# A convolution branch whose first transform stage goes from 128-row matmuls to pairs of 64-row matmuls, and whose middle stage goes from 16 points over four frequencies to 32 points over two

## The chip, the cores and the metric

The kernel runs on one core of a Trainium2 chip. The metric is the time of one execution on the device in microseconds (us). Three executions of the kernel before took 1200.62, 1201.41 and 1201.98 us; the median, 1201.41 us, is the time that the changed kernel is held against. The core has a matrix engine (TensorE, PE in the rows, with its weight loads listed as PEld), a vector engine (DVE), a scalar engine (ACT), GpSimd (POOL) and a sync engine (SP), which here only issues transfers. The matrix engine holds a weight block of up to 128 rows by 128 columns, streams a moving operand past it and adds the products into a bank of PSUM. Each engine works through its own instructions in order and waits on semaphores for the others.

## The reference: what is computed

The input x has 2048 positions and 576 channels. Four layers are applied, A, B, A, B, each as x + layer(layernorm(x)):

```python
def _A_ref(x, ...):                      # real part of a 2-D DFT, as matmuls
    a, b = x @ hid_re.T, x @ hid_im.T
    return seq_re @ a - seq_im @ b

def _B_ref(q, k, v, shift_k, ssm_k, ssm_D):
    k_shift = short causal convolution of k (4 taps per channel)
    kv = k_shift * v
    y = long causal convolution of kv with ssm_k, per channel, 2048 taps (by FFT)
    return q * (y + kv * ssm_D)
```

In layer B only q, the normalized x, depends on the layers before. kv, ssm_k and ssm_D are inputs, and both B layers use the same ones. So the long convolution ("the branch") is worked out once, from the inputs alone, and both B layers read its result.

## The kernel before

Every float32 operand of a matmul is split into a rounded high part and a low remainder (`split`: ACT writes the high part, line 91, and DVE the low part, line 92). Each product is three matmuls: high by high, high by low, low by high. All go through the helper `mm`, line 74, so that rows of PE all name L74.

**The main line.** The first layer A runs in `layer` over 128 steps (g, tb, k): real or imaginary sequence matrix, one of four blocks of 512 output positions, one of 16 blocks of 128 input positions. A step is 14 matmuls with 512 moving columns: 12 into four banks named s (four channel blocks, three matmuls each) and 2 into the bank rm for the last 64 channels. Its matrix block (`c_mat`, 256 KB) is loaded two steps ahead and split by ACT and DVE. In the first 16 steps x is normalized too (`get_x0`, ACT, DVE and a power on POOL). After each pair of g the channel transform runs (`hidden`, `finish`), 27 matmuls of 288 columns to a half row block. A second layer A follows, part of it by a seven-product scheme (`strassen`), and its channel transform ends the program.

**The branch** (`branch`, a generator) is interleaved with the steps of the first layer A. It has four stages:

1. the short convolution and the product with v on DVE (`convolve`, lines 386 and 391, and line 419);
2. the first transform stage (`f1_products`). Position n is written 16p + j, with p the partition and j one of 16 residues. For each j and each of two sources (kv and ssm_k) the 128 values over p are multiplied by a 128 x 128 cosine matrix and a 128 x 128 sine matrix, in two halves of 288 channels. That gives 128 frequencies in real and imaginary part, for each residue. The result is copied from PSUM by ACT (line 436) and stored to DRAM, `t_d`, by ACT's queue (line 437);
3. the middle stage (`mid_*`): 64 times, 128 rows of `t_d` are loaded (four frequencies, 16 residues, two parts), a 16-point transform over the residues is applied as one block-diagonal 128 x 128 matrix, the spectrum of kv is multiplied by that of ssm_k, and an inverse 16-point transform is applied and stored to `v_d`;
4. the last transform stage (`i2_products`): 32 times, 128 frequencies back to 128 positions, to `yb_d`.

Stage 2 has 32 units (16 j by 2 sources). A unit has two halves of the channels, and a half has two banks, c = 0 for cosine and c = 1 for sine, with three matmuls of 288 columns in each and a copy by ACT behind each:

```python
for c in range(2):
    ps = bank()
    mm(ps[:, :HD], fc[:, c, :], xf[0][:, cs], True, False)
    mm(ps[:, :HD], fc[:, c, :], xf[1][:, cs], False, False)
    mm(ps[:, :HD], fc[:, 2 + c, :], xf[0][:, cs], False, True)
    stored[:] = [nc.scalar.activation(so[:, c, :], ps[:, :HD], AF.Copy).ins]
```

The banks come from a ring of three (`bank`), which the channel transform and the other stages of the branch use as well. The units are doled out over the steps 0 to 42 of the first layer A by a fixed formula (`want`, from `F1_16` and `F1_END`); each unit is named in the program behind a step, and a scheduler in the build mixes the matmuls of neighbouring parts. The weights `fc` of a unit (256 KB for each j) come through POOL's queue (line 165) into a ring of five; the first one comes through SP's queue as float32 (lines 408 and 409). Loads of `c_mat`, x, k, v and ssm_k go through SP's queue. All constants are made on the host by `_constants`, and `kernel` lays the inputs out.

Of the kernel before, what the change touches and what calls it, by code (L numbers as in the profile page):

```python
# [10 lines left out]
F32 = mybir.dt.float32  # L11
FR = mybir.dt.float32r
AF = mybir.ActivationFunctionType
OP = mybir.AluOpType

P = 128
S = 2048
D = 576
J = S // P
TB = 4  # L20
NT = 512
HD = D // 2
NC = 4
REM = D - NC * P
EPS = 1e-5
# [22 lines left out]
KP = 4  # L48
H = 2 * P
WIDE = 2 * NT  # L50
# [14 lines left out]
def fnet_h3_kernel(ctx: ExitStack, tc: tile.TileContext, x, c_mat, w_re, w_im, k_pad, v, shift_k,  # L65
                   ssm_k, ssm_d, f1c, i2c, midc, out):
    nc = tc.nc
# [3 lines left out]
    dr = ctx.enter_context(tc.tile_pool(name="dr", bufs=1, space=bass.MemoryType.DRAM))  # L71

    def mm(ps, lhsT, rhs, first, last, more=False):
        nc.tensor.matmul(ps, lhsT, rhs, start=first, stop=last, skip_group_check=more)  # L74

    def bank():
        return psp.tile([P, NT], F32, tag="b", bufs=3, name="bk")

    acc4 = [psp.tile([P, NT], F32, tag=f"s{i}", name=f"s{i}") for i in range(4)]
    last_pair = [acc4[2:]]  # L80
# [24 lines left out]
    def flat(words, dt, name):  # L105
        return sb.tile([P, words], dt, tag=name, name=name)

# [3 lines left out]
    def region_b(dt, name):  # L111
        return sb.tile([P, 6 * WIDE], dt, tag="rb", name=name)
# [9 lines left out]
    ring = {}  # L122

    def lay(t, at, *sizes):

        for name, words, n in sizes:
            ring.setdefault(name, Ring()).tiles.extend(t[:, at + i * words:at + (i + 1) * words] for i in range(n))
            at += n * words
        assert at <= t.shape[1], (at, t.shape, sizes)
        return at  # L130
# [5 lines left out]
    def two(v):  # L136
        return v.rearrange("p (a n) -> p a n", a=2)
# [17 lines left out]
    anchor, made, rounded, pows, biased, halved, added, evac, parted, stored = [], [], [], [], [], [], [], [], [], []  # L155
# [3 lines left out]
    def load_after(dst, src):  # L159
        with tc.issue_after(anchor[-1]):  # L160
            return nc.sync.dma_start(dst, src).ins

    def load_fr(dst, src):
        with tc.issue_after(pows[-1]):
            nc.gpsimd.dma_start(dst, src)
# [25 lines left out]
        made.append(nc.vector.tensor_tensor(t[:, D + REM:], y[:, :NC * P], h[:, :NC * P], OP.subtract).ins)  # L191
        return t

    t_d = [dr.tile([P, J, 2, 2, HD], F32, name=f"t{h}") for h in range(2)]
    v_d = [dr.tile([P, J, 2, HD], F32, name=f"vd{h}") for h in range(2)]
    yb_d = [dr.tile([P, D], F32, name=f"yb{j}") for j in range(J)]
    xa_d = [dr.tile([P, D], F32, name=f"xa{j}") for j in range(J)]
# [141 lines left out]
    def quads(v):  # L339
        return v.rearrange("p (a q) -> p a q", a=4)  # L340

    def branch():
        f1r = region_b(FR, "f1r")
        lay(f1r, 0, ("xf", 2 * D, 3), ("fc", 4 * P, 5))
        at = lay(flts, SC_AT + CRAW * NT, ("so", D, 4), ("land", D, 3))
        lay(flts, at, ("craw", NT, 1))
        f1f = region_a(F32, "f1f")
        ks = f1f[:, :KR * 2 * D]
        lay(f1f, KR * 2 * D, ("wt", 2 * D, 2), ("rp", 2 * D, 2))
        tmp = f1f[:, 8 * 2 * D:]  # L350
        wt, rows, landed, fcs = [], {}, {}, {}
# [9 lines left out]
        def load_k(upto):  # L361
            while k_loaded[0] < min(upto, (J + 4) // 2):
                i = k_loaded[0]
                at = i % KR * 2 * D
                nc.sync.dma_start(ks[:, at:at + 2 * D],
                                  bass.AP(tensor=k_pad.tensor, offset=k_pad.offset + 2 * i * D,
                                          ap=[[J * D, P], [1, 2 * D]]))
                k_loaded[0] += 1

        def k_rows(row):  # L370
# [27 lines left out]
        def f1_loads(upto):  # L398
            while loads[0] < min(upto, len(todo)):
                j, src = todo[loads[0]]  # L400
                loads[0] += 1
                if j not in fcs:
                    fcs[j] = quads(ring["fc"]())
                    if pows:
                        load_fr(fcs[j], f1c[j])
                    else:
                        raw = quads(tmp[:, :4 * P])
                        nc.sync.dma_start(raw, f1c[j])
                        nc.scalar.activation(fcs[j], raw, AF.Copy)
                landed[j, src] = ring["land"]()  # L410
                nc.sync.dma_start(landed[j, src], (ssm_k if src else v)[:, j, :])
                if src and j == 0:
                    nc.sync.dma_start(tmp[:1, D:], ssm_d[None, :])
# [13 lines left out]
        def f1_products(j, src, xf, fc):  # L427
            for hf in range(2):
                so = two(ring["so"]())
                cs = slice(hf * HD, (hf + 1) * HD)  # L430
                for c in range(2):
                    ps = bank()
                    mm(ps[:, :HD], fc[:, c, :], xf[0][:, cs], True, False)
                    mm(ps[:, :HD], fc[:, c, :], xf[1][:, cs], False, False)
                    mm(ps[:, :HD], fc[:, 2 + c, :], xf[0][:, cs], False, True)
                    stored[:] = [nc.scalar.activation(so[:, c, :], ps[:, :HD], AF.Copy).ins]  # L436
                nc.scalar.dma_start(t_d[hf][:, j, :, src, :], so)
                yield

        conv, made_ops, split_up = convolve(), 0, []  # L440
        for n, (j, src) in enumerate(todo):
            f1_loads(n + 1)
            if n < 2:
                yield
            split_up.append((j, src, f1_split(j, src), fcs[j]))
            products = f1_products(*split_up.pop(0)) if len(split_up) > (1 if n < F1_LAG else 2) else iter(())
            if n:
                f1_loads(n + 3)
            later = [m for m in range(n + 1, len(todo)) if todo[m][1] == 0 and 7 * (todo[m][0] // 2 + 1) > made_ops]
            for half in range(2):  # L450
                next(products, 0)
                if later and n > 2:
                    left = 7 * (todo[later[0]][0] // 2 + 1) - made_ops
                    for _ in range(-(-left // (2 * (later[0] - n) - half)) if left > 0 else 0):
                        next(conv)
                        made_ops += 1
                yield
        next(conv, 0)
        for left_over in split_up:
            yield from f1_products(*left_over)  # L460
        m1 = region_b(FR, "mid")
        kk_at = SC_AT + CRAW * NT + 4 * D
        at = lay(m1, 0, ("df", 2 * D, 3), ("mc", 4 * P, 1))
# [6 lines left out]
        at = lay(m1, at, ("yf", D, 2))  # L470
        fc_at = at
        at = lay(flts, SC_AT + CRAW * NT, ("res", D, 2))
# [76 lines left out]
        rows = [f[2] for f in feeds if f[0]]  # L549
        landed, halves, fcs, yfs = {}, {}, {}, []  # L550

        def load_feed(i):
            if i < len(feeds):
                kind, hf, q = feeds[i]
                landed[i] = ring["land"]()
                load_after(landed[i], v_d[hf][:, q].rearrange("p c d -> p (c d)") if kind else
                           t_d[hf][4 * q:4 * q + 4].rearrange("q j c s d -> (q j c) (s d)"))

        def load_fc(k):
            if k < len(rows):  # L560
# [10 lines left out]
        for i in range(3):  # L571
            load_feed(i)
        yield 0
        for i in range(2):
            split_feed(i)
            load_feed(i + 3)
# [173 lines left out]
    for n, whole in layer(get_x0, lambda j: x[:, j, :], done0, pending):  # L750
# [3 lines left out]
        if (whole or whole is not None and n % J < J - 1) and n <= F1_END and not part:  # L754
            at = n if whole else n - 0.5
# [25 lines left out]
        m = n - PREP  # L781
# [138 lines left out]
    cs, done = {}, []  # L920
# [68 lines left out]
    for n, whole in layer(get_x1, lambda j: xb_d[j], done1, pending, 1):  # L989
# [12 lines left out]
        if n == STATIC:  # L1002
            t7.append(region_a(FR, "t7"))
            at = lay(flts, SC_AT + CRAW * NT, ("csum", WIDE, 3), ("rems", 2 * REM, 2))
# [50 lines left out]
def _r11(a):  # L1055
    u = np.ascontiguousarray(a, np.float32).view(np.uint32).astype(np.uint64)
    u = (u + 0x7FF + ((u >> 12) & 1)) & 0xFFFFF000
    return u.astype(np.uint32).view(np.float32)


def _parts(a):
    h = _r11(a)
    return h, _r11(a - h.astype(np.float64))


def _constants():
    p, q, j, r = np.arange(P), np.arange(P), np.arange(J), np.arange(J)
    n = (16 * p[None, :, None] + j[:, None, None]) * (4 * q[None, None, :] + 1) % 8192
    ang = 2 * np.pi * n / 8192
    f1 = [_parts(np.cos(ang)), _parts(-np.sin(ang))]  # L1070
    f1c = np.stack([f1[0][0], f1[1][0], f1[0][1], f1[1][1]], axis=2)
    at = ang.transpose(0, 2, 1)
    i2 = [_parts(np.cos(at) / S), _parts(-np.sin(at) / S)]
    i2c = np.stack([i2[0][0], i2[1][0], i2[0][1], i2[1][1]], axis=2)
    th = 2 * np.pi * (j[:, None] * r[None, :] % J) / J
    f2 = np.zeros((4, J, 2, 2, 4, J))
    i1 = np.zeros((2, 4, J, 4, J, 2))
    c, s = np.cos(th), np.sin(th)
    for a in range(4):
        f2[a, :, 0, 0, a, :] = c  # L1080
        f2[a, :, 1, 0, a, :] = s
        f2[a, :, 0, 1, a, :] = -s
        f2[a, :, 1, 1, a, :] = c
        i1[0, a, :, a, :, 0] = c.T
        i1[1, a, :, a, :, 0] = -s.T
        i1[0, a, :, a, :, 1] = s.T
        i1[1, a, :, a, :, 1] = c.T
    m = [*_parts(f2.reshape(P, P)), *_parts(i1.reshape(P, P))]
    return f1c, i2c, np.stack(m, axis=1)

# [35 lines left out]
```

## Time and profile before

| | |
|---|---|
| median of three executions | 1201.41 us (1200.62 to 1201.98) |
| the profiled execution, first to last instruction | 1198.9 us |
| its granted matrix clock | 0.998 of full speed |
| PE busy | 1178.8 us, 98% of the span, 6320 matmuls |
| PEld busy | 1025.6 us, 86% |
| DVE busy | 839.6 us, 70% |
| ACT busy | 665.4 us, 55% |
| first transform stage, first to last matmul | 6.8 to 200.8 us |

The profiled execution's own time, as far as the page gives it, is its span of 1198.9 us; the median of the executions is 2.5 us above that. A row of the groups view names the line, engine and operation, then output <- inputs, the tile and the shapes with the count, then busy time in us and mean duration of one in ns, then the engine's idle time ahead of these instructions with what ended most of it. Matmuls are pipelined: a matmul's duration reaches from its start until its result is out, and the next one starts long before that. So the spacing of starts, not the duration, says what a matmul costs in a row of them. In the timeline a row is start, length and a run of like instructions (x9: nine of them).

### The profile page before, as it was taken

Reading aid. Unit: us, or ns where it says so; the run is one execution under the profiler, and the core shown is the slowest. Engines: PE = TensorE matmul, PEld = TensorE weight load, DVE = VectorE, ACT = ScalarE, POOL = GpSimd, SP = SyncE. Lnnn points to the kernel's source line nnn. Section 1 sums busy time; section 2 is a strip of 40 time slices with the busy share of each in tenths; the row PEclk is TensorE's granted clock in tenths of the full one; section 3 lists DMA queues with packets and bytes.
Section 4 is the critical chain, followed back from the end, with each engine's and each line's share of the span. In section 5 each row is a group of like instructions: output and inputs, shape, how many; then the busy total and the mean of one; then the engine's idle time right before and its main releaser. Section 6 shows DMA issues by size and latency. Waiting matters only on the chain.

```text
span 1198.9 us, 18258 instructions
## 1 busy us (share of the span) xinstructions
PE 1178.8 (98%) x6320; PEld 1025.6 (86%) x6320; DVE 839.6 (70%) x1498; ACT 665.4 (55%) x1335; POOL 74.7 (6%) x116
## 2 busy tenths in 40 slices
PE   7999999999999999999999999999999999999997
PEld 6888888988888888888988898888888888789997
DVE  7899983679777677675347766775776777774764
ACT  7855665679877668774435666544444445450210
POOL 2210000000000000001101121000000000001111
PEclk9999999999999999999999999999999999999999
DMA  9869898546766667648967686872682677795621
GB/s 356 292 225 311 282 299 243 188 133 184 219 188 199 213 172 210 193 134 267 291 207 233 221 255 212 272 267 71 216 283 72 208 285 260 238 338 156 218 88 40
DMA packets 146110, 261.95 MB, mean 218 GB/s; under 512 B 15841, under 2 KB 44769, under 8 KB 146018
## 3 DMA queue, kind: packets, MB, share of 16 engines
q1 hardware_dynamic: 102674, 205.58, 53.9%
q10 hardware_dynamic: 36432, 42.63, 10.2%
q0 software_dynamic: 6912, 12.59, 3.9%
q8 instruction: 49, 0.80, 0.3%
q14 instruction: 43, 0.35, 0.1%
HBM read 194.09 MB, written 66.65 MB: 217 GB/s over the span
## 4 chain that ended last, share of the span: by engine, by line
PE 89%; ACT 4%; DVE 3%; DMA 2%; issue 2%; POOL 0%; ACTq 0%; SPq 0%; POOLq 0%; DVEq 0%
PE s L74 50%; PE bk L74 34%; PE rm L74 5%; ACT flts L490 2%; ACT mid L490 1%; DMA flts<-in_c_mat 1%; DVE mats L92 0%; ACT mats L91 0%; ACT u L91 0%; DMA flts<-in_ssm_k 0%; DMA ph<-in_c_mat 0%; DMA wd<-w 0%; DVE u L92 0%; DVE mid L496 0%; DVE f1f L386 0%
## 5 line engine op out<-in xcount | busy, mean ns | idle before, releaser
L74 PE MATMUL s<-mats 128*128 128x512 f32 x2088 | 535.0, 391 | 1.2 <-DVE u L92 0.5
L74 PEld LDWEIGHTS s<-mats 128*128 128x128 f32 x2088 | 380.0, 188 | 70.1 <-DVE u L92 1.1
L92 DVE TENSOR_TENSOR mats<-flts,mats 128x512 fp32r<-128x512 f32 x206 | 140.9, 688 | 63.8 <-ACT mats L91 63.3
L91 ACT ACTIVATE mats<-flts 128x512 fp32r<-128x512 f32 x206 | 128.5, 628 | 84.5 <-PE bk L74 32.3
L74 PEld LDWEIGHTS bk<-mid 128*128 128x128 f32 x768 | 116.2, 188 | 21.7 <-ACT flts L490 8.1
L74 PE MATMUL bk<-mid 128*128 128x288 f32 x768 | 132.5, 299 | 2.2 <-ACT flts L490 2.0
L74 PE MATMUL bk<-w,u 128*128 128x288 f32 x864 | 120.9, 296 | 0.3 <-ACT flts L490 0.3
L74 PEld LDWEIGHTS bk<-w,u 128*128 128x128 f32 x864 | 117.4, 188 | 4.0 <-ACT flts L490 1.9
L496 DVE TENSOR_TENSOR mid<-flts,mid 128x576 fp32r<-128x576 f32 (+1 forms) x149 | 93.5, 628 | 35.2 <-ACT mid L490 32.7
L490 ACT ACTIVATE flts<-bk 128x288 f32<-128x288 f32 x160 | 62.2, 405 | 90.1 <-PE bk L74 81.0
L74 PE MATMUL rm<-mats 128*128 128x512 f32 x304 | 94.9, 391 | 0.0
L490 ACT ACTIVATE flts<-flts 64x288 f32<-64x288 f32 x192 | 85.0, 443 | 5.5
L490 ACT ACTIVATE mid<-flts 128x576 fp32r<-128x576 f32 (+1 forms) x148 | 80.3, 575 | 6.0 <-DMA flts<-t 3.0
L436 ACT ACTIVATE flts<-bk 128x288 f32<-128x288 f32 x128 | 49.3, 410 | 49.9 <-PE bk L74 41.3
L74 PE MATMUL bk<-f1r 128*128 128x288 f32 x384 | 64.2, 300 | 7.7 <-ACT f1r L91 7.6
L74 PEld LDWEIGHTS bk<-f1r 128*128 128x128 f32 x384 | 59.0, 191 | 14.8 <-ACT f1r L91 8.6
L280 DVE TENSOR_TENSOR flts<-flts,bk 128x288 f32<-128x288 f32 x48 | 21.8, 453 | 67.6 <-PE bk L74 67.6
L74 PE MATMUL bk<-mats 128*128 128x288 f32 (+1 forms) x376 | 67.8, 317 | 0.0
L74 PEld LDWEIGHTS rm<-mats 128*128 128x128 f32 x304 | 56.9, 188 | 12.3 <-DVE flts L266 0.3
L74 PE MATMUL s<-t,mats 128*128 128x512 f32 x264 | 64.9, 389 | 0.0
L177 POOL TENSOR_TENSOR flts<-flts 128x1 f32<-128x1 f32 x35 | 29.4, 841 | 522.2 <-DVE flts L176 522.2
L74 PE MATMUL bk<-mats,t 128*128 128x288 f32 (+1 forms) x368 | 59.3, 303 | 0.0
(145 smaller groups left out, 1505.4 us busy)
## 6 DMA issues: line engine op xcount, KB each, us to landing
flts<-in_c_mat SPq DMA_DIRECT2D x148, 256.0 KB, 3.8
ph<-in_c_mat SPq DMA_DIRECT2D x54, 512.0 KB, 4.5
t<-flts ACTq DMA_DIRECT2D x64, 288.0 KB, 4.5
flts<-in_c_mat SPq DMA_DIRECT2D x30, 512.0 KB, 5.3
flts<-t SPq DMA_DIRECT2D x53, 288.0 KB, 2.9
vd<-flts ACTq DMA_DIRECT2D x64, 144.0 KB, 2.3
flts<-vd SPq DMA_DIRECT2D x32, 288.0 KB, 4.5
mid<-in_i2c POOLq DMA_DIRECT2D x32, 256.0 KB, 4.9
```

What stands on the lines that cost most here:

```text
L74: nc.tensor.matmul(ps, lhsT, rhs, start=first, stop=last, skip_group_check=more)
L91: a = nc.scalar.activation(h, src, AF.Copy).ins
L92: return a, nc.vector.tensor_tensor(l, src, h.bitcast(F32), OP.subtract).ins
L177: pows.append(nc.gpsimd.tensor_tensor(rs, ve, mhalf, OP.pow).ins)
L280: added[:] = [nc.vector.tensor_tensor(r[:, cs], r[:, cs], ps[:, :HD], OP.add).ins]
L436: stored[:] = [nc.scalar.activation(so[:, c, :], ps[:, :HD], AF.Copy).ins]
L490: last_act.append(nc.scalar.activation(*args, **kw).ins)
L496: nc.vector.tensor_tensor(l, src, h.bitcast(F32), OP.subtract)
```

## The change

Stage 2 now writes the position as n = 32p + w, with p from 0 to 63 and 32 residues w. For each residue the transform has 64 points: 64 rows are contracted, and the 128 output columns hold 64 frequencies in real and imaginary part. Two residues, j and j + 16, stand in the lower and the upper 64 partitions of the same tile: the host puts the rows of k, v and ssm_k in that order (`by_half`). A half of a unit is now six matmuls of 64 rows, 128 weight columns and 288 moving columns. They alternate between rows 0 to 63, with sums in one bank, and rows 64 to 127, with sums in another; the two banks are taken together, and both copies by ACT come behind the six matmuls. The count of matmuls, copies and stores stays as it was. In the build the matmuls of 64 rows carry a tile size of 64 x 128 and a tile position of row 0 or row 64; all the others carry 128 x 128 at row 0.

The weights of a unit halve from 256 to 128 KB. `t_d` has its 32 residues in place of 16 residues by two parts; a store writes as many rows of the same length, further apart, and a load of the middle stage reads the same number of rows as before. The middle stage covers two frequencies with 32 residues and two parts, again 128 rows, so that only the contents of its matrices change. The last stage reads its frequencies in another order, which is put into its constants. k is stored with its overlapping rows written out, so that a plain slice reads it.

```diff
-    t_d = [dr.tile([P, J, 2, 2, HD], F32, name=f"t{h}") for h in range(2)]
+    t_d = [dr.tile([P, 2 * J, 2, HD], F32, name=f"t{h}") for h in range(2)]
...
-        lay(f1r, 0, ("xf", 2 * D, 3), ("fc", 4 * P, 5))
+        lay(f1r, 0, ("xf", 2 * D, 3), ("fc", 2 * P, 5))
...
-                    fcs[j] = quads(ring["fc"]())
+                    fcs[j] = two(ring["fc"]())
                     if pows:
                         load_fr(fcs[j], f1c[j])
                     else:
-                        raw = quads(tmp[:, :4 * P])
+                        raw = two(tmp[:, :2 * P])
                         nc.sync.dma_start(raw, f1c[j])
...
                 so = two(ring["so"]())
                 cs = slice(hf * HD, (hf + 1) * HD)
-                for c in range(2):
-                    ps = bank()
-                    mm(ps[:, :HD], fc[:, c, :], xf[0][:, cs], True, False)
-                    mm(ps[:, :HD], fc[:, c, :], xf[1][:, cs], False, False)
-                    mm(ps[:, :HD], fc[:, 2 + c, :], xf[0][:, cs], False, True)
-                    stored[:] = [nc.scalar.activation(so[:, c, :], ps[:, :HD], AF.Copy).ins]
-                nc.scalar.dma_start(t_d[hf][:, j, :, src, :], so)
+                ps = [bank() for _ in range(2)]
+                for n, (a, b) in enumerate(((0, 0), (0, 1), (1, 0))):
+                    for i in range(2):
+                        rows = slice(i * HP, (i + 1) * HP)
+                        mm(ps[i][:, :HD], fc[rows, a, :], xf[b][rows, cs], n == 0, n == 2)
+                for i in range(2):
+                    stored[:] = [nc.scalar.activation(so[:, i, :], ps[i][:, :HD], AF.Copy).ins]
+                nc.scalar.dma_start(t_d[hf][:, j::J, src, :], so)
...
-                           t_d[hf][4 * q:4 * q + 4].rearrange("q j c s d -> (q j c) (s d)"))
+                           t_d[hf][4 * q:4 * q + 4].rearrange("m j s d -> (m j) (s d)"))
...
-    n = (16 * p[None, :, None] + j[:, None, None]) * (4 * q[None, None, :] + 1) % 8192
-    ang = 2 * np.pi * n / 8192
-    f1 = [_parts(np.cos(ang)), _parts(-np.sin(ang))]
-    f1c = np.stack([f1[0][0], f1[1][0], f1[0][1], f1[1][1]], axis=2)
+    n = (32 * (p % HP) + J * (p // HP))[None, :, None] + j[:, None, None]
+    ang = 2 * np.pi * (n * (4 * q[None, None, :HP] + 1) % 8192) / 8192
+    f1 = _parts(np.stack([np.cos(ang), -np.sin(ang)], axis=3).reshape(J, P, P))
+    f1c = np.stack(f1, axis=2)
...
+    def by_half(m):
+        return m.reshape(HP, 2, *m.shape[1:]).transpose(1, 0, *range(2, m.ndim + 1)).reshape(m.shape)
...
-        "v": a["B_v"].reshape(P, J, D),
+        "v": by_half(a["B_v"].reshape(P, J, D)),
...
-        "ssm_k": a["B_ssm_k"].T.reshape(P, J, D),
+        "ssm_k": by_half(a["B_ssm_k"].T.reshape(P, J, D)),
```

More of the change, by code (lines that the diff above doesn't have):

```diff
@@ L16 @@
 P = 128
+HP = P // 2
 S = 2048
@@ L364, in load_k @@
                 at = i % KR * 2 * D
-                nc.sync.dma_start(ks[:, at:at + 2 * D],
-                                  bass.AP(tensor=k_pad.tensor, offset=k_pad.offset + 2 * i * D,
-                                          ap=[[J * D, P], [1, 2 * D]]))
+                nc.sync.dma_start(ks[:, at:at + 2 * D], k_pad[:, 2 * i * D:2 * (i + 1) * D])
                 k_loaded[0] += 1
@@ L1066, in _constants @@
 def _constants():
-    p, q, j, r = np.arange(P), np.arange(P), np.arange(J), np.arange(J)
+    p, q, j = np.arange(P), np.arange(P), np.arange(J)
+    n = (32 * (p % HP) + J * (p // HP))[None, :, None] + j[:, None, None]
+    ang = 2 * np.pi * (n * (4 * q[None, None, :HP] + 1) % 8192) / 8192
+    f1 = _parts(np.stack([np.cos(ang), -np.sin(ang)], axis=3).reshape(J, P, P))
+    f1c = np.stack(f1, axis=2)
     n = (16 * p[None, :, None] + j[:, None, None]) * (4 * q[None, None, :] + 1) % 8192
-    ang = 2 * np.pi * n / 8192
-    f1 = [_parts(np.cos(ang)), _parts(-np.sin(ang))]
-    f1c = np.stack([f1[0][0], f1[1][0], f1[0][1], f1[1][1]], axis=2)
-    at = ang.transpose(0, 2, 1)
+    at = (2 * np.pi * n / 8192).transpose(0, 2, 1)
+    at = at[:, np.concatenate([[2 * g, 2 * g + 1, HP + 2 * g, HP + 2 * g + 1] for g in range(HP // 2)])]
     i2 = [_parts(np.cos(at) / S), _parts(-np.sin(at) / S)]
     i2c = np.stack([i2[0][0], i2[1][0], i2[0][1], i2[1][1]], axis=2)
-    th = 2 * np.pi * (j[:, None] * r[None, :] % J) / J
-    f2 = np.zeros((4, J, 2, 2, 4, J))
-    i1 = np.zeros((2, 4, J, 4, J, 2))
+    w = np.arange(2 * J)
+    th = 2 * np.pi * (w[:, None] * w[None, :] % (2 * J)) / (2 * J)
+    f2 = np.zeros((2, 2, 2 * J, 2, 2, 2 * J))
+    i1 = np.zeros((2, 2, 2 * J, 2, 2, J, 2))
     c, s = np.cos(th), np.sin(th)
[L1079 to L1087, printed above, removed]
+    for a in range(2):
+        f2[a, 0, :, 0, a, :] = c
+        f2[a, 1, :, 0, a, :] = s
+        f2[a, 0, :, 1, a, :] = -s
+        f2[a, 1, :, 1, a, :] = c
+    th = 2 * np.pi * (j[:, None] * j[None, :] % J) / J
+    c, s = np.cos(th), np.sin(th)
+    for a in range(2):
+        for b in range(2):
+            i1[0, a, b::2, b, a, :, 0] = c
+            i1[1, a, b::2, b, a, :, 0] = -s
+            i1[0, a, b::2, b, a, :, 1] = s
+            i1[1, a, b::2, b, a, :, 1] = c
     m = [*_parts(f2.reshape(P, P)), *_parts(i1.reshape(P, P))]
@@ L1107 @@
         "w_im": a["A_dft_hid_im"].T,
-        "k_pad": np.pad(a["B_k"][0], ((3, 1), (0, 0))),
-        "v": a["B_v"].reshape(P, J, D),
+        "k_pad": by_half(np.stack([np.pad(a["B_k"][0], ((3, 1), (0, 0)))[J * p:J * p + J + 4].reshape(-1)
+                                   for p in range(P)])),
+        "v": by_half(a["B_v"].reshape(P, J, D)),
         "shift_k": a["B_shift_k"].T,
-        "ssm_k": a["B_ssm_k"].T.reshape(P, J, D),
+        "ssm_k": by_half(a["B_ssm_k"].T.reshape(P, J, D)),
         "ssm_d": a["B_ssm_D"],
```

## The prediction

> **What bounds the kernel now.** I read the page first: the engines' shares and the slices.
>
> ```profile
> PE 1178.8 (98%) x6320; PEld 1025.6 (86%) x6320; DVE 839.6 (70%) x1498; ACT 665.4 (55%) x1335; POOL 74.7 (6%) x116
> ...
> PE   7999999999999999999999999999999999999997
> ...
> DVE  7899983679777677675347766775776777774764
> ```
>
> PE is at work through the whole span, DVE for about two thirds of it. But DVE stands at 8 or 9 in slices two to six (30 us each), and that is where the first transform stage lies. The chain of work that ended last says whether PE's time is the path:
>
> ```profile
> PE 89%; ACT 4%; DVE 3%; DMA 2%; issue 2%; POOL 0%; ACTq 0%; SPq 0%; POOLq 0%; DVEq 0%
> ```
>
> It is, for 89%. So a microsecond of PE added to any stage, or taken from it, is about a microsecond of time, as long as no other engine runs full in that stage. Next the stage itself, by windows, first of all instructions and then of those that touch the branch's tile f1r (columns: PE, PEld, DVE, ACT, POOL in us with counts, clock, DMA share, GB/s):
>
> ```profile
> 15.00:90.00 75.00, 74.24 (x355) 61.59 (x354) 66.81 (x131) 57.79 (x121) 13.85 (x18) 1.00 0.83 287
> 90.00:180.00 90.00, 89.99 (x487) 78.48 (x487) 82.77 (x98) 53.77 (x121) 3.69 (x7) 1.00 0.94 297
> 180.00:202.00 22.00, 22.00 (x123) 19.40 (x122) 7.45 (x11) 13.74 (x31) 0.53 (x1) 1.00 0.76 219
> ```
>
> ```profile
> 15.00:90.00 75.00, 14.01 (x81) 12.35 (x81) 4.51 (x6) 4.07 (x6) 2.69 (x5) 1.00 0.83 287
> 90.00:180.00 90.00, 37.01 (x228) 34.65 (x229) 16.18 (x22) 14.20 (x21) 3.69 (x7) 1.00 0.94 297
> 180.00:202.00 22.00, 9.39 (x60) 8.82 (x60) 1.75 (x3) 1.35 (x2) 0.00 (x0) 1.00 0.76 219
> ```
>
> PE is busy throughout, at full clock. DVE is busy 66.81 + 82.77 = 149.6 of the 165 us from 15 to 180 us, so a faster PE finds 15.4 us of idle DVE there and no more; from 180 us on DVE is free. 309 of the stage's 384 matmuls stand in the tight part, 60 in the free one.
>
> **What a matmul costs today.** Groups by shape, two pieces of the chain, and the timeline of PE and of its loads:
>
> ```profile
> L74 PE MATMUL s<-mats 128*128 128x512 f32 x2088 | 535.0, 391 | 1.2 <-DVE u L92 0.5 <-ACT mats L188 0.3 <-DVE mats L191 0.3
> ...
> L74 PE MATMUL bk<-f1r 128*128 128x288 f32 x384 | 64.2, 300 | 7.7 <-ACT f1r L91 7.6
> ...
> L74 PEld LDWEIGHTS bk<-f1r 128*128 128x128 f32 x384 | 59.0, 191 | 14.8 <-ACT f1r L91 8.6 <-ACT flts L436 1.1
> ```
>
> ```profile
> 146.98 2.74 PE s L74 x12
> ...
> 1076.20 115.02 PE bk L74 x866
> ```
>
> ```profile
> 165.65 0.56 PE L74 MATMUL bk<-f1r 128*128 128x288 f32 x3
> 166.05 0.39 PE L74 MATMUL s<-mats 128*128 128x512 f32 x1
> 166.28 0.56 PE L74 MATMUL bk<-f1r 128*128 128x288 f32 x3
> 166.68 1.32 PE L74 MATMUL s<-mats 128*128 128x512 f32 x5
> ```
>
> ```profile
> 85.55 0.30 PEld L74 LDWEIGHTS bk<-f1r 128*128 128x128 f32 x2 [0.57 <-ACT f1r L91]
> ```
>
> By spacing, a matmul of 512 columns costs 2.74 / 12 = 0.228 us and one of 288 columns 115.02 / 866 = 0.133 us, though their durations are 0.391 and 0.300: each starts while the one before it still has 0.163 us to run (0.391 - 0.228). In the stage the spacing is the same: three f1r matmuls from 165.65 to 166.05 take 0.40, the one of 512 columns behind them 0.23, the next three 0.40. Going from one width to the other costs nothing. So the stage costs PE 384 x 0.133 = 51.1 us. The last row shows a load by itself: after a wait two loads follow each other, and 0.30 less the duration of one, 0.19, gives 0.11 us from load to load. Every matmul has its own load, today hidden under the matmul before it, 0.11 under 0.133.
>
> **The change, part by part.** *Pairs.* As many matmuls as before, 384, each as long as before in columns, but two of them on different rows may stream together. In the order in which the changed kernel issues its matmuls they stand in 75 blocks between the others, some of odd length (24 blocks of three); counted in pairs, with one over in each odd block, they fill 207 places. If loads and matmuls of the two row halves both run side by side, the stage costs 207 x 0.133 = 27.5 us: gain 23.5. If the matmuls do but the loads queue at 0.11, it costs 384 x 0.11 = 42.2: gain 8.8. If nothing overlaps, 0. I take 16, the middle of the upper two, since no row favours either. The Trainium skill, "TensorE: Matmul & The Clock Gate", section "Measured speedup vs the span model", has four row tiles reach 3.07 of the possible 4; the same share of two would be 1.53, an estimate from that page, and a gain of 51.1 - 51.1 / 1.53 = 17.7, so the sum by it would be 2 us lower. No run here shows it yet.
>
> *Change of tile shape.* All 6320 matmuls of today have the form 128*128, so the overlap of 0.163 is shown between matmuls of one shape alone. 75 blocks make 150 changes between 128 rows and 64 rows. Lower end: 0, as for the change of width. Upper end: the array runs empty first and the next load starts only then, 0.163 + 0.11 = 0.273, or 41 us in all. I take 0.163, 150 x 0.163 = 24.5 us. The two ends lie far apart, and the row nearest to a change of shape is the run-out of the 512-column matmul that stands at these very borders; no row shows matmuls of two shapes under way at once, and the load of 0.11, shorter than the run-out, can lie under it. The Trainium skill, "TensorEngine Tiling (Array Packing)", section "Key Properties", says that changing the tiling mode, other than changing the tile, drains the engine; by it the sum with 24.5 to 41 stands and the one with 0 falls. No run here shows that either.
>
> *Banks.* Two banks are taken at once, of three. The next pair's second bank is then the first of this pair, which ACT must have copied:
>
> ```profile
> L436 ACT ACTIVATE flts<-bk 128x288 f32<-128x288 f32 x128 | 49.3, 410 | 49.9 <-PE bk L74 41.3 <-DMA t<-flts 8.1
> ```
>
> ```profile
> PEld bk L74 <- ACT flts L436: 1.1, 4, 0.4
> ```
>
> Today PE's loads wait 1.1 us in all for these copies. A later half needs the copy (0.41) finished; where eight matmuls of 512 columns lie between, 1.8 us, that is time enough. In the six blocks of 9 or 12 matmuls nothing lies between: 6 x 0.41 = 2.5 us. Ends: 0, and 64 halves x 0.41 = 26 if ACT is always late. I take 2.5, since ACT is idle 49.9 us before these copies. Behind a waiting matmul stands all of the main line.
>
> *Transfers and constants, all at nothing.* Weights of 128 in place of 256 KB: 15 loads on POOL's queue, well ahead of use, and one on SP's, ahead of the first ssm_k; the chain at the start goes over that ssm_k load, not over the weights' copy, so at most some tenths of a us are gained. k, v and ssm_k move the same bytes in the same count of rows; if they were late, DVE's convolution would wait. The stores to `t_d` write the same rows further apart; four buffers cover them, and if they landed later, ACT's wait for them (8.1 us above) would grow inside ACT's idle time first. The middle and last stages keep every instruction: no change.
>
> **Sum.** 24.5 - 16 + 2.5 = +11.0 us on the profiled 1198.9, so a span of 1209.9. The median lies 2.5 us above the span: 1212. A difference below 0.2% (2.4 us) can't be told from none in this kernel.
>
> **Rivals.** *The array doesn't empty (faster).* Then the changes cost 0 and PE could save 23.5. For it: the free change of width above. Against it: that is one shape. But in the 165 tight microseconds 309 / 384 of it, 18.9 us, meet 15.4 us of idle DVE; that idle time is made of waits and won't be used up, so I count 10, plus 30 x 0.133 = 4 after 180 us, less 2 for banks: -12, 1189. It decides from a change cost of 0.09 us downwards: (16 - 2.5) / 150.
>
> *The array doesn't empty and loads queue (faster).* -8.8 + 2.5 = -6.3: 1195. For it speaks the row of two loads 0.11 apart; against it, both are loads of all 128 rows, and the trace has none of half the rows.
>
> *Emptying with the load behind it (slower).* 41 - 16 + 2.5 = +27.5: 1229. For it: in today's trace a load starts where the matmul before it starts, so one held back holds back its load. Against it: at 0.11 it is shorter than the run-out of 0.163 and may lie beside it.
>
> *The change doesn't do what it says.* Pairs run one after the other, gain 0: +2.5 without emptying, 1204; 24.5 + 2.5 = +27 with it, 1228. Nothing in the rows excludes it: every matmul of the trace starts after the one before it has streamed, 0.133 or 0.228 apart.
>
> **How the numbers follow.** Forecast (emptying at 0.163, some overlap) 0.36; its own range is 24.5 + 2.5 - 23.5 = +3.5 to 24.5 + 2.5 - 8.8 = +18.2, 1205 to 1220. No emptying, all side by side 0.24; no emptying, loads queued 0.12; emptying with loads behind 0.14; no overlap 0.14, half of it each way. Slower: 0.36 + 0.14 + 0.07 and half of the 0.07 at 1204, 0.60; faster: 0.24 + 0.12 less 0.01 whose bank waits eat the gain, 0.35; the rest, 0.05, is the same. The range takes in 1189 and 1229 with some 3 to 5 us for the banks and for DVE: 1186 to 1234. Outside stay a DVE that gives way wholly and waits for banks at most halves.
>
> **What would show it.** In the profile after, f1r matmuls carry 64-row shapes. Emptying shows as the first f1r matmul of a block starting about 0.39 us, not 0.23, after the 512-column matmul before it, and the first s matmul some 0.3, not 0.13, after the last f1r one; pairs as two starts a few ns apart and the next pair 0.13 (loads side by side) or 0.22 later (loads queued); banks as PE's or PEld's wait on ACT L436, today 1.1 us, grown to some 3.5; DVE as bound by its window from 15 us on being over 95% busy in a shorter stage. Everything after the stage should be shifted and otherwise equal. The prediction is wrong if block borders keep a spacing of 0.13 and 0.23; then the stage ends before today's 202 us, not after it.

## The result and the profile after

The changed kernel takes 1209.01 us (median of four, 1208.29 to 1210.95) against 1201.16 us beside it: a ratio of 1.0071, with a 95% interval of 1.0057 to 1.0086. It is 7.9 us slower. The forecast was slower, 1212 us, with 1205 to 1220 as the range of its own case.

The page, first the engines, then the slices of PE and PEld, then the group of the first transform stage:

```profile
PE 1189.2 (99%) x6320; PEld 1004.4 (83%) x6320; DVE 840.7 (70%) x1498; ACT 664.1 (55%) x1335; POOL 76.2 (6%) x116
...
PE   8999999999999999999999999999999999999997
PEld 5776667998888888888988898888888888789997
...
L75 PE MATMUL bk<-f1r 64*128 64x288 f32 x384 | 53.3, 333 | 5.9 <-ACT f1r L408 5.7
```

The span is 1207.0 us, 8.1 more than before. The stage's matmuls now have the form 64*128 and are busy for 53.3 us where they were busy for 64.2, and yet PE as a whole is busy 10.4 us longer. The weight loads have lost time in the first slices (5776667), which is the stage. The windows, of all instructions, show where the span grew (columns as before: PE, PEld, DVE, ACT, POOL, clock, DMA share, GB/s):

```profile
180.00:202.00 22.00, 22.00 (x120) 15.23 (x120) 7.96 (x12) 11.84 (x29) 0.00 (x0) 1.00 0.77 244
202.00:210.00 8.00, 7.89 (x45) 5.51 (x44) 3.49 (x5) 5.43 (x13) 0.53 (x1) 1.00 0.79 243
210.00:1207.00 997.00, 985.12 (x5332) 860.05 (x5330) 673.48 (x1231) 531.16 (x1047) 51.44 (x80) 1.00 0.63 205
```

The last 997 us hold 985.12 us of PE with 5332 matmuls. The window of the same length in the kernel before:

```profile
202.00:1199.00 997.00, 985.18 (x5331) 859.90 (x5329) 673.28 (x1231) 530.39 (x1047) 51.80 (x80) 1.00 0.65 205
```

So everything behind the stage is the same work at the same pace, 8 us later. All of the loss lies in the stage.

A border of the stage, in the timeline of PE and then of PEld (start, length, run of instructions, idle time ahead):

```profile
154.61 0.61 PE L75 MATMUL rm<-mats 128*128 128x512 f32 x2
155.15 1.06 PE L75 MATMUL bk<-f1r 64*128 64x288 f32 x9
156.15 0.96 PE L75 MATMUL s<-mats 128*128 128x512 f32 x3
```

```profile
154.38 0.41 PEld L75 LDWEIGHTS rm<-mats 128*128 128x128 f32 x2
155.15 0.83 PEld L75 LDWEIGHTS bk<-f1r 64*128 64x128 f32 x9 [0.35 <-issue]
156.14 0.53 PEld L75 LDWEIGHTS s<-mats 128*128 128x128 f32 x3 [0.17 <-issue]
```

The second rm matmul starts at 154.61 + 0.228 = 154.84. The next load starts at 155.15, 0.32 later, though no semaphore holds it: the view names "issue" as the reason. Its matmul is listed from 155.15 on too, but can only stream once the load is done. The first two matmuls of a block last 0.397 to 0.398 and the later ones 0.292, so a load that nothing hides takes 0.106, and the stream starts at 155.26. Without a change of shape it would have streamed at 154.84 + 0.228 = 155.07. The loss is 0.19 to 0.20 us: 0.09 until the load may start, and the load itself, which is no longer hidden. The way back costs the same: the last load of a block and the next load of the main line stand apart by an idle 0.17 with the same name. Over all borders of the profile the median is 0.195 us going in and 0.193 coming out.

### The profile page after: what moved, and what is told of

Its sections match the earlier page's. It is cut to its first block, busy times and chain, and to the rows that moved or that the text cites. A ratio compares the mean times of both kernels' runs of the same rounds, so it can differ in the third digit from the quotient of the medians.

```text
span 1207.0 us, 18256 instructions
## 1 busy us (share of the span) xinstructions
PE 1189.2 (99%) x6320; PEld 1004.4 (83%) x6320; DVE 840.7 (70%) x1498; ACT 664.1 (55%) x1335; POOL 76.2 (6%) x116
## 4 chain that ended last, share of the span: by engine, by line
PE 72%; ACT 4%; DVE 2%; DMA 2%; issue 1%; ACTq 0%; SPq 0%; POOLq 0%; DVEq 0%
PE s L75 39%; PE bk L75 29%; PE rm L75 4%; ACT flts L490 2%; ACT mid L490 1%; DMA wd<-w 1%; DMA t<-ud 1%; DMA flts<-in_c_mat 1%; ACT mats L92 0%; ACT u L92 0%; DVE mid L496 0%; DVE mats L93 0%; DVE flts L511 0%; DVE flts L509 0%; DVE flts L510 0%
## 5 line engine op out<-in xcount | busy, mean ns | idle before, releaser
L75 PE MATMUL s<-mats 128*128 128x512 f32 x2088 | 545.1, 396 | 0.6 <-DVE u L93 0.5
L490 ACT ACTIVATE flts<-bk 128x288 f32<-128x288 f32 x160 | 62.1, 405 | 89.5 <-PE bk L75 77.1
L436 ACT ACTIVATE flts<-bk 128x288 f32<-128x288 f32 x128 | 46.9, 408 | 58.7 <-PE bk L75 58.6
L75 PEld LDWEIGHTS bk<-f1r 64*128 64x128 f32 x384 | 34.9, 188 | 33.2 <-issue 15.2
L75 PE MATMUL bk<-f1r 64*128 64x288 f32 x384 | 53.3, 333 | 5.9 <-ACT f1r L408 5.7
```

What stands on the lines that cost most here:

```text
L436: stored[:] = [nc.scalar.activation(so[:, i, :], ps[i][:, :HD], AF.Copy).ins]
L490: last_act.append(nc.scalar.activation(*args, **kw).ins)
```

## The experiments

**Changes of shape alone.** The kernel before, without any pairs; one matmul in each of 64 later steps gets the 64-row shape.

```diff
-            mm(ps[NC], xr, c[1], False, last)
+            rows = slice(0, P // 2 if blocks == TB and n >= 64 else P)
+            mm(ps[NC], xr[rows], c[1][rows], False, last)
```

> The kernel before, with no pairs, but in the 64 steps from 64 on the last matmul of each step (512 columns, into rm) contracts only rows 0 to 63 and so has the 64-row shape. Left out by it: the low part of the matrix block against the last 64 channels, for the upper half of the positions of those steps. That is 64 matmuls of another shape, 128 changes of shape, and nothing else is changed. Theory A (each change of shape empties the array and then loads, 0.195 us as the borders of the changed kernel show): 128 x 0.195 = 25 us more than before, 1226 us. With the forecast's 0.163: 21 us, 1222. Theory B (a change is free, the loss comes from lost pairs, banks or transfers): 1201, as before.

Measured: 1222.72 us against 1200.70, ratio 1.0180 (1.0166 to 1.0194). That is 22.0 us for 128 changes, 0.172 us each. The timeline of its weight loads over one step:

```profile
665.66 2.57 PEld L74 LDWEIGHTS s<-mats 128*128 128x128 f32 x12 [0.24 <-issue]
668.27 0.19 PEld L74 LDWEIGHTS rm<-mats 128*128 128x128 f32 x1
668.81 0.18 PEld L74 LDWEIGHTS rm<-mats 64*128 64x128 f32 x1 [0.35 <-issue]
669.24 0.30 PEld L74 LDWEIGHTS s<-mats 128*128 128x128 f32 x2 [0.25 <-issue]
```

From 665.66 to 669.24 the 14 matmuls of the step take 3.58 us; at 0.228 each they would take 3.19. Two changes cost 0.39, 0.195 each, as at the stage's borders. Over the whole run a change costs a little less, 0.172. The traces show where the rest goes: away from the changes, the waits of PE's loads behind 215 us add up to 18.5 us in the kernel before and to 13.2 here. These 5.3 us more than cover the 3.0 by which 22.0 falls short of 128 x 0.195 = 25.0: stops take the place of waits that PE had anyway. A free change (theory B) is out.

**The new layout with the old shape.** Weights of all 128 rows, zero in the other half.

```diff
-                        rows = slice(i * HP, (i + 1) * HP)
-                        mm(ps[i][:, :HD], fc[rows, a, :], xf[b][rows, cs], n == 0, n == 2)
+                        mm(ps[i][:, :HD], fc[:, 2 * i + a, :], xf[b][:, cs], n == 0, n == 2)
...
+    f1c = np.zeros((J, P, 4, P), np.float32)
+    for i in range(2):
+        for a in range(2):
+            f1c[:, i * HP:(i + 1) * HP, 2 * i + a] = f1[a][:, i * HP:(i + 1) * HP]
```

> The changed kernel with its new layout, residues, middle stage and bank order, but each matmul of the first stage takes all 128 rows, with weights that are zero in the other half (256 KB again). No change of shape, and no pair streams side by side. Theory A: the stage costs PE what it did before, so 1201 us within 2. Theory C (the layout costs: stores further apart, two banks at once, the order of the copies): the loss of 8 us stays, in part or whole, 1203 to 1209.

Measured: 1201.51 against 1200.70, ratio 1.0004 (0.9995 to 1.0013). The layout, the stores that lie further apart, the two banks taken at once and the changed middle stage cost nothing that can be told from none. What is left for the loss is the shape of the matmuls and what follows from it. For the banks the run speaks only at the old pace, 0.8 us for a half unit: its loads wait 1.3 us for ACT's copies, 1.1 in the kernel before.

**One row half after the other.** The six matmuls of a half unit are kept together, but three of one half come ahead of three of the other; the three banks are taken in turn.

```diff
+        taken[0] += 1
+        return banks[taken[0] % 3]
...
-                for n, (a, b) in enumerate(((0, 0), (0, 1), (1, 0))):
-                    for i in range(2):
-                        rows = slice(i * HP, (i + 1) * HP)
+                steps = [(n, i, a, b) for n, (a, b) in enumerate(((0, 1), (0, 0), (1, 0))) for i in (1, 0)]
+                steps.sort(key=lambda s: -s[1])
+                for at, (n, i, a, b) in enumerate(steps):
+                    rows = slice(i * HP, (i + 1) * HP)
+                    with behind(*(recent[-1:] if at else recent)):
                         mm(ps[i][:, :HD], fc[rows, a, :], xf[b][rows, cs], n == 0, n == 2)
```

> The changed kernel with the three matmuls of rows 64 to 127 ahead of the three of rows 0 to 63 in each half unit, kept together in this order, and the three banks taken in turn. So 64 blocks in place of 75, but only one place in each block where two halves can stream together: 64 x 5 = 320 places of 0.133 us in place of 242. Theory A: +78 x 0.133 = +10.4 for lost pairs and -11 blocks x 2 x 0.195 = -4.3, 1215 us. If pairs gain nothing: 1209 - 4.3 = 1205.

Measured: 1201.97 against 1200.70, ratio 1.0007 (0.9998 to 1.0016). Both expectations failed, the 1215 for lost pairs by 13 us. A block in its timeline:

```profile
152.64 0.67 PE L77 MATMUL bk<-f1r 64*128 64x288 f32 x6
153.24 0.97 PE L77 MATMUL s<-mats 128*128 128x512 f32 x3
```

Six matmuls, from the first start to the last end, take 0.67 us. One load (0.106), two spacings of 0.133 and a last duration of 0.29 make 0.66: three places, not five. So the pairs were not lost. The fourth matmul, the first of the other half, starts 0.01 us after the first, ahead of the second and third. So PE does not start its matmuls strictly in the order in which the program issues them: with three of one half ahead of three of the other, the two row halves still take theirs side by side, and they need not alternate. My count of places by neighbours (242 in the changed kernel) was wrong. Counted by block, as the larger of the two halves' numbers, the changed kernel fills 231 places and this run 192. The trace of the changed kernel bears this out: of its 75 blocks 71 last as long as this count says, within 0.03 us; the other four are two ahead of 11 us and the two blocks of twelve, which wait for a bank.

**Pairs kept.** The same without the sort (one line less), so the halves alternate.

> The changed kernel with the six matmuls of each half unit kept together and alternating, the low part first, and the three banks taken in turn so that the half begins with the bank that is freed last: 64 blocks in place of 75 and 192 places in place of 242, all in pairs. Theory A: -50 x 0.133 = -6.7 and -11 x 2 x 0.195 = -4.3, so 1198 us, a little under the kernel before (1201). If the changes cost nothing and lost pairs were all of the loss: the stage would cost 25.5 us where it cost 51.1, 1185 or less. If waits for the two banks matter: over 1203.

Measured: 1200.57 against 1200.70, ratio 0.9995 (0.9986 to 1.0004), level with the kernel before. Against the changed kernel (1.0071) that is 0.76% or 9.1 us. By the corrected count, 231 - 192 = 39 places give 5.2 us and 11 blocks fewer give 22 x 0.195 = 4.3, 9.5 in all. So near a fit is partly chance: 1.5 us for the two blocks of twelve (below) come on top, and against them stand waits of PE's loads for the operands of s that come back, 1.7 and 0.9 us in the two longest rows, 0.4 and 0.2 in the changed kernel. The run before, with one row half after the other, lies 1.4 us above this one, and the two intervals overlap. A block of this run, in the timeline of PE:

```profile
154.59 0.39 PE L77 MATMUL rm<-mats 128*128 128x512 f32 x1
154.91 0.66 PE L77 MATMUL bk<-f1r 64*128 64x288 f32 x6
155.50 0.50 PE L77 MATMUL rm<-mats 128*128 128x512 f32 x1
```

The first rm matmul has streamed at 154.59 + 0.228 = 154.82; the second one streams from 155.50 + 0.106 = 155.61. Between them lie 0.79 us for a half unit. Six matmuls of the old shape took 6 x 0.133 = 0.80. Three pairs gain no more than the two changes of shape around them cost. This is the whole case in one block.

**Written order, and blocks of twelve.** If a block of three pairs breaks even, longer blocks should win. In the program each call of the branch gives out half a unit. The first run issues all matmuls up to step 42 strictly in the program's order, the second also names both halves of a unit together.

```diff
+        with behind(*(recent[-1:] if strict else [])):
...
+            want -= want % 2
```

> The kernel of the run before with kept pairs, but all matmuls up to step 42 of the first layer A are issued strictly in the order in which the program names them: 61 blocks of 64-row matmuls (58 of six, 3 of twelve). It is the yardstick for the next run. Three blocks fewer: -1.2 us; three waits for a bank, +0.6 each; what the strict order itself costs is open, 0 to 5 us: 1200 to 1206.

> The same in strict order, but the two halves of a unit are named one right behind the other, so that 33 blocks (31 of twelve, 2 of six) stand in place of 61: 56 changes of shape fewer, 56 x 0.195 = 10.9 us gained. Theory D (banks): four banks are wanted in a block and three are there; the second half's first bank must be emptied by ACT first, 0.17 until the last result is out plus 0.41 for the copy, about 0.6 us in which PE stands still, 31 x 0.6 = 18.6 us lost. Sum: 8 us more than the strict order with blocks of six. Theory E (the wait for the bank is hidden): 11 us less than it, about 1190, which would beat the kernel before.

Measured: 1207.22 against 1199.73 for the written order, ratio 1.0061 (1.0044 to 1.0079), a little over the range given; 1223.82 for blocks of twelve, ratio 1.0204 (1.0187 to 1.0221). Longer blocks lose 16.6 us more, twice the 8 us expected. The loads' waits for ACT's copies, in the written order:

```profile
PEld bk L78 <- issue: 14.2, 36, 1.4
...
PEld bk L78 <- ACT flts L445: 6.4, 4, 2.5
```

and in blocks of twelve:

```profile
PEld bk L78 <- ACT flts L445: 34.9, 30, 3.0
PEld bk L78 <- issue: 9.2, 26, 0.4
```

In blocks of twelve PE's loads wait 30 times, 1.16 us each and not 0.6, for a bank to be copied out: 34.9 against 6.4 is 28.5 us lost, 56 changes fewer give back 10.9, and 17.6 is close to the 16.6 measured. The shorter "issue" row shows the borders that went away. One of the waits, with the two copies ahead of it:

```profile
102.82 0.71 ACT L445 ACTIVATE flts<-bk 128x288 f32<-128x288 f32 x2 [1.62 <-PE bk L78]
...
103.58 0.43 PEld L78 LDWEIGHTS bk<-f1r 64*128 64x128 f32 x6 [1.03 <-ACT flts L445]
```

The load starts 0.05 us after the second copy has ended (102.82 + 0.71 = 103.53); the expectation had counted one copy, 0.41. Why the second is waited for was not traced. A block of twelve should pay with four banks in place of three; beside the four of s and the one of rm, that was not tried.

The written order itself missed its range for two reasons that its trace shows. Its three blocks of twelve wait 2.5, 1.0 and 2.5 us for a bank, where 0.6 each was expected. And in the last of these waits, which ends at 151.9 us, PE's granted clock falls (columns as before, the clock third from the end):

```profile
150.00:155.00 5.00, 3.07 (x11) 2.40 (x12) 4.25 (x6) 3.25 (x7) 0.51 (x1) 0.64 0.35 107
```

From 155 to 160 us it is 0.67. Lost shares of 0.36 and 0.33 over 5 us each make at most 3.4 us. The two executions with a mean clock of 0.998 take 1205.5 and 1205.6 us, inside the range; the two with 0.995 and 0.997 take 1209.4 and 1208.8. In blocks of twelve all four have 0.994 to 0.997, so part of the 16.6 is the clock, and the fit with 17.6 is partly chance.

## Why the prediction was right, and where its terms were off

*What bounds the kernel.* Right: PE's loss in the stage is the loss of the whole, and the 997 us behind it did not change.

*Pairs.* The forecast left it open whether the loads run side by side, and took a gain of 16 between 8.8 and 23.5. They do: two loads and two matmuls of a pair start within 0.01 us of each other, and the next pair follows 0.13 later. The upper end was the right case, but its 207 places were too few: 21 of the 75 blocks hold one row half alone, so 231 places were filled, and the gain was (384 - 231) x 0.133 = 20.3 us. The term was 4 us too small. The order of the blocks said so already: 30 blocks are of odd length, and 20 of them, not 24, are blocks of three; 17 of these hold three matmuls of one half, which the count of lengths did not look at. The Trainium skill, "TensorE: Matmul & The Clock Gate", section "Measured speedup vs the span model", gives 3.07 for four tiles, from which the forecast estimated 1.53 for two. Two tiles did better here: within a block of pairs they come to 2, one pair in each 0.133 us.

*Change of tile shape.* That changes stop the array was right, and they were the largest term. Its size was 0.163 in the forecast and is 0.195 by the borders, 150 x 0.195 = 29.2 us where 24.5 stood. The step that failed is "the load of 0.11, shorter than the run-out, can lie under it". The run-out that is paid is shorter: the next shape's load starts 0.09 us after the streaming, ahead of the listed end of the matmul before it (155.15 against 155.22 in the border shown). The load comes behind it, in full. So it is the rival "emptying with the load behind it", with a smaller emptying. The Trainium skill, "TensorEngine Tiling (Array Packing)", section "Key Properties", says that a change of tiling mode drains the engine while a change of tile does not. The traces agree with both halves of it: 0.195 us at each change of mode, none from row half to row half.

*Banks.* 2.5 us were forecast, with a row that grows from 1.1 to some 3.5 as the sign. The row after:

```profile
PEld bk L75 <- ACT flts L436: 3.7, 11, 0.4
```

The number came out, for another reason. Nine of the 11 waits stand where a block begins, such as this one:

```profile
102.50 0.43 PEld L75 LDWEIGHTS bk<-f1r 64*128 64x128 f32 x3 [0.36 <-ACT flts L436]
```

They last 0.34 us on average, as long as the stops that the view names "issue" (15.2 us in 42, and 0.35 in the border above). So they are the stop at a change of shape, listed under the copy's name, and are paid for in the 29.2. The other two stand inside the two blocks of twelve:

```profile
140.79 1.82 PE L75 MATMUL bk<-f1r 64*128 64x288 f32 x12
...
141.95 0.43 PEld L75 LDWEIGHTS bk<-f1r 64*128 64x128 f32 x3 [0.34 <-ACT flts L436]
```

Six places would take 0.106 + 5 x 0.133 + 0.29 = 1.06 us; this block takes 1.82, 0.76 more, since the last three matmuls wait and then run without a partner. Two such blocks cost 1.5 us. That the term is small rests on blocks of six with main-line work between them, as blocks of twelve showed.

*Transfers and constants.* Nothing, as forecast (ratio 1.0004). The first matmul of the stage starts at 5.7 us and not at 6.8, but no gain follows from it. The first four s matmuls, in the changed kernel and in the kernel before:

```profile
7.81 2.07 PE L75 MATMUL s<-mats 128*128 128x512 f32 x4
```

```profile
9.21 1.32 PE L74 MATMUL s<-mats 128*128 128x512 f32 x4
```

Matmuls of 512 columns start about 0.43 us apart until 13 us in the changed kernel, and 0.23 apart from 9.9 us on in the kernel before; why the slow pace lasts longer was not traced. Nor do the halved weights alone give the early start: with pairs kept they are halved too, and the first matmul, there one with the low part of its operand, starts at 6.7 us.

*The sum.* 29.2 - 20.3 + 1.5 = +10.4 us against 8.1 in the span. The 2.3 us that are left over are covered by waits that PE had anyway, as in the run with changes alone. In the kernel before, PE's loads waited 3.3 us for other engines between 15 and 210 us; in the changed kernel 0.4 us of such waits are left beside the borders and the blocks of twelve. That brings the sum to 7.5, within 1 us of the 8.1. The forecast's +11.0 came from a gain and a cost that were each some 4 to 5 us too small and cancelled, and its bank term from blocks that mostly did not wait. The direction was reasoned; that 1212 came so near to 1209 was luck.

*The rivals.* "The array doesn't empty", with its loads side by side or queued, fell with the run of changes alone. DVE never became the bound, since PE did not get faster. "The change doesn't do what it says" fell with the pairs in the trace.

## What to carry to other kernels

Packing two matmuls of half height side by side halved their time on PE here, but each change between the packed and the full shape cost a fixed stop and an uncovered weight load. Before writing it, count the blocks that the order makes, not only the matmuls: here one block had to gain 0.39 us to break even, and three pairs of 288 columns gain 0.40. Longer blocks would need more PSUM banks, since a wait for a copy out of PSUM (1.16 us here) costs more than the two changes it saves (0.39). And before a wait is put down to the engine that its row names, look at where it stands: nine of 11 "waits for ACT" were the stop at a change of shape.

## What had not been expected of the hardware

- The two row halves of TensorE took their matmuls independently within a block: three of one half ahead of three of the other took 0.67 us, like three pairs.
- Loads for the two halves ran at the same time, each 0.106 us, so that a packed stream at 288 columns kept 0.133 us for a pair.
- A change of shape cost the same in both directions, 0.195 and 0.193 us. At none of the borders of the trace did a weight load start ahead of the change, while within a shape each load lies under the matmul before.
- In the written order PE's granted clock fell during a wait of 2.5 us, to 0.64 and 0.67 in the windows of 5 us from 150 and 155 us on.
